# Dummy TensorE products behind the first score products, and another place in the order for the check of two counts

## The chip, the cores and the metric

One core of a Trainium2 chip runs the whole program. The metric is the device time of one execution in microseconds (us): 548.85 us, the median of three runs (548.45 to 549.34).

## The reference

Attention over 2 x 8 heads, 768 tokens, head size 64, with a window: token t sees the first `n_global` (8) tokens and the last `n_local` (96), with a linear bias by distance. Behind it stand two mixture layers on the 1536 x 512 result: `r * (relu(xk W_k)^2 W_v)` with `r = sigmoid(xr W_r)` and `xk`, `xr` mixed from each token and the one before it, then `x + relu(norm(x) W_1) W_2`. All in float32 accuracy; the weights arrive as 64-bit words that the kernel turns into float32 itself.

```python
scores = scale * np.matmul(q, k.transpose(0, 1, 3, 2))
scores = np.where(keep, scores + bias, -1000000000.0)
a = softmax(scores);  x = a @ v
x = r * ((np.maximum(xk @ w_k, 0) ** 2) @ w_v)
return x + np.maximum(norm(x) @ w_ch1, 0) @ w_ch2
```

## The kernel before, in words

The two counts `n_global` and `n_local` are data. The fast path holds for counts up to 8 and 96; `outside_band` (L75 to L88, with `counts`, L64) works out on VectorE (DVE) in small instructions whether they lie outside, and a branch at the very end of the program (L1368 to L1372) reads the flag and would run a general path. `constants` (L249) makes the bias tables from the same counts: a first part for the first block ahead of everything, the rest in four steps (L287 to L298).

The order of the work is not written by hand. Methods of `Fast` hand operations to a planner (`Plan`, L110): each operation has one or more engines with an assumed cost in ns, the cells it reads and writes, the buffers ("rooms") it needs, a due time, and, in `behind`, other operations after which alone it may be placed. `play` (L143) then simulates the engines: again and again it takes, of all operations that could go, the one that can start first, and among those that can start at the same moment the one with the earliest due time (L176). The order that comes out is each engine's instruction queue. On the chip each engine works its queue strictly in that order; `behind` puts no wait of its own into the program, only data and buffers do. So a change of a cost, or one more operation, can change the order of everything planned after it.

The stages, in order of time:

- Attention (to about 133 us). Work goes in half blocks: 128 queries, four heads. `plan_turn` (L431) transposes q and k on TensorE (PE, L446) into PSUM banks 3 and 7; DVE scales q (L453), ScalarE (ACT) copies k (L345). `plan_scores` (L471) makes the scores of a half block with four products (L492) into two of the banks 0 to 2; DVE adds the bias and finds the least value of a row (L503, "least"), ACT takes the exponent (L509). `plan_weighted` (L514) transposes the result (L527), ACT copies it to SBUF (L345), and PE multiplies with v (L542). `plan_out` (L549) scales by the sums: GpSimd (POOL, L566, L570), DVE (L567), PE (L577), ACT (L345), DVE (L583). The scores of half block i are due at 6 + 5 i us of the plan.
- Weight words are converted all along: SP loads (L598), ACT or POOL take the high word (L349, L345), DVE works in L601, L602 and L603, then a high and a low part follow on ACT (L609) and POOL or DVE (L613).
- The first mixture, six groups of 256 tokens: `plan_r` (L728), `plan_k` with the keys products (L764), `plan_v` with the values products (L801 to L803) into banks 4 and 5 (bank 6 in the last group) and DVE L815 that takes them out. `self.mixed` (L937) is the planner's number of the last keys product of the last group.
- The second mixture from about 276 us: `plan_norm` (L834 to L881), `plan_up` (PE L1056, DVE L1064) and `plan_down` (PE L1150 to L1152, DVE L1156 and L1166).

At the start PE has nothing to do until q arrives; `warm_up` (L240) gives it nine products of ones. The check of the counts is the last operation handed to the planner (L942): one DVE operation, cost 3000, no cells, no rooms, nothing in `behind`, and the latest due time of all.

Of the kernel before, what the change touches and what calls it, by code (L numbers as in the profile page):

```python
# [16 lines left out]
P = 128  # L17
B, H, S, D = 2, 8, 768, 64
# [5 lines left out]
NG = NTOK // GT  # L24
# [18 lines left out]
PAIRS = 8  # L43
UP, LEAD = 15.6, 10.0
WARM = 9
SCALE = 0.125
BIG = 2.0**38
SM_EPS = 1e-9
# [3 lines left out]
def slope(h):  # L52
    return 2.0 ** (-8.0 * (h + 1) / H)
# [162 lines left out]
class Fast:  # L216
# [23 lines left out]
    def warm_up(self):  # L240
# [4 lines left out]
        self.nc.vector.memset(y.bitcast(F32), 1.0)  # L245
        for _ in range(WARM):
            self.nc.tensor.matmul(ps, y[:, 0:P], y, start=True, stop=True)
# [52 lines left out]
    def query_scale(self):  # L300
        self.qs = self.t([P, 4, 1], "qs")
        for h in range(H):
            self.nc.gpsimd.memset(self.qs[(h % 2) * D : (h % 2 + 1) * D, h // 2, :], -SCALE / slope(h))

# [166 lines left out]
    def plan_scores(self, i):  # L471


        nc, p = self.nc, self.plan
        n, hf = i // 2, i % 2
        c0, c1 = self.cols(n)
        w = c1 - c0
        banks = [Room(f"b{(2 * i + e) % 3}", 1, lambda e=e: self.bank((2 * i + e) % 3)) for e in range(2)]
        S = lambda k: banks[k % 2].tile[:, 0 : 2 * w].rearrange("p (j w) -> p j w", j=2)[:, k // 2, :]
        due = self.due(i)  # L480
        if hf == 0:
            self.sm[n] = self.room("sm", 3, [P, H])
        sm = self.sm[n]
        tp, mn = self.tp[i], _ = Part([self.TP, self.token(f"tp{i % 3}", 1)], lambda t, _: t[:, i % 3]), self.room("mn", 3, [P, 4])
        sides = [n % 2] if n % NB == 0 else [0, 1, 2]
        o = P + MAXG if n % 2 else 0
        s = hf if n == 0 else 0

        def scores(e):
            for k in range(4):  # L490
                r, c = slice((k % 2) * D, (k % 2 + 1) * D), 2 * hf + k // 2
                nc.tensor.matmul(S(k), self.qT(n)[r, c], self.kT()[r, c, c0:c1], start=True, stop=True)  # L492

        reads = self.sides(n, s, "qT", n % 2)
        for x in sides:
            reads += self.sides(n, s, "kT", x)
        p.op({"PE": 3.4 * w}, scores, reads, [("S", i)], banks + [self.Q, self.K], due, mode="rows")
        for x, k in enumerate((0, 2, 1, 3)):
            h = 4 * hf + k

            def least(e, k=k, h=h):
                bias = self.nb0 if n % NB == 0 else self.nb[:, o : o + WW]
                nc.vector.tensor_tensor_reduce(  # L503
                    tp.tile[:, k, 0:w], S(k), bias, slope(h), 3.0e38, ALU.add, ALU.min, mn.tile[:, k : k + 1]
                )

            def exp(e, k=k, h=h):
                t = tp.tile[:, k, 0:w]
                nc.scalar.activation(t, t, AF.Exp, bias=mn.tile[:, k : k + 1], scale=-1.0, accum_out=sm.tile[:, h : h + 1])  # L509

            p.op({"DVE": 165 + 1.31 * w}, least, [("S", i), ("nb", n % NB > 0)], [("tp", i, k)], [tp, mn, banks[k % 2], self.bias], due + 1 + x)
            p.op({"ACT": 385 + 0.86 * w}, exp, [], [("tp", i, k), ("sm", n, h)], [tp, mn, sm], due + 1.5 + x)

    def plan_weighted(self, i):  # L514

# [367 lines left out]
    def first(self, last):  # L883
        self.plan = p = Plan(CLOCK)
        C = 4 * (2 * P + MAXG)
        self.V, self.sm, self.tp, self.O, self.X, self.k2 = {}, {}, {}, {}, {}, {}
        self.K = self.room("b0h", 1, [P, C + 1024])
        self.Q = self.room("b0l", 1, [P, 4, 512])
        self.U = self.room("u", 1, [P, 2, 512])
        self.VW = self.room("h1", 1, [P, 3, 2, H, D])  # L890
        self.TP = self.room("t0l", 1, [P, 3, 4, GT])
        self.Y = self.room("yy", 1, [P, 2, 2, 512])
        early = self.room("s1", 1, [P, 4, 512, 2], I32)
        bias = self.constants()
        self.bias = Room("ln", 1, lambda: self.nb)
        with self.tc.manual_schedule(engines=ORDERED):
            self.warm_up()
            next(bias)
            self.query_scale()
            self.small_params()  # L900
            rooms = [self.token("rt", 2), self.token("rt", 2), self.token("e", 2)]
            for ns in (350, 500, 800, 900):
                p.op({"DVE": ns}, lambda e: next(bias, None), (), [("nb", True)], rooms, self.due(1))
            for n in range(NBLK):
                self.plan_loads(n)
                self.plan_values(n)
                self.plan_turn(n)
                for i in (2 * n, 2 * n + 1):
                    self.plan_scores(i)
                    self.plan_weighted(i)  # L910
                self.plan_out(n)
            self.plan_weights()
            self.j = 0
            for j, i in enumerate(self.order[0:12]):
                raw = Part([early], lambda t, j=j: t[:, j - 2]) if j in (2, 3) else None
                self.plan_weight(("m1", i), self.src[i], lambda i=i: self.place(i), CONV0 + CONV1 * j, raw=raw)
            for g in range(EG):
                self.plan_r(g, self.due(4 * g + 3) + 45)
            r3 = self.r_op
            self.plan_k(0, K0, K0 - 6)  # L920
            k0 = self.k_op
            for j, i in enumerate(self.order[12:]):
                behind = [r3] if i in (16, 17) else [k0] if i in (14, 15) else []
                self.plan_weight(("m1", i), self.src[i], lambda i=i: self.place(i), CONV2 + CONV3 * j, behind)
            end = self.due(24) + 8
            at = {g: end + 24 * (g - 1) for g in range(NG + 1)}
            self.plan_k(1, at[1], at[1] - 8)
            self.k1 = self.k_op
            self.plan_v(0, at[1] + 12)
            for g in range(1, NG):  # L930
                if g + 1 < NG:
                    self.plan_k(g + 1, at[g + 1], at[g + 1] - 15)
                self.plan_v(g, at[g + 1] + 12 if g + 1 < NG else at[g] + 24)
                if g == 1:
                    self.free = self.x_op
                if g == NG - 2:
                    self.mixed = self.k_op  # L937
                if EG <= g + 1 < NG:
                    self.plan_r(g + 1, at[EG] - 12 + 12 * (g + 1 - EG))
                    self.gone = self.r_op  # L940
            self.plan_second(at[NG])
            p.op({"DVE": 3000}, lambda e: last(), due=at[NG] + 150)  # L942
            self.trace = p.play()

    def plan_second(self, start):
# [451 lines left out]
```

## Time and profile before

| | us |
|---|---|
| median of three runs | 548.85 |
| the profiled execution, as timed | 548.74 |
| its span, first to last instruction | 546.9 |
| PE busy with matmuls | 523.7 |
| DVE busy | 403.0 |
| ACT busy | 288.9 |
| POOL busy | 272.9 |

The span is what the trace covers; the timed execution is 1.84 us longer. Matmuls are pipelined and their ends are modelled, so a busy PE isn't PE at its peak. The page has a row with the clock that TensorE was granted, as a share of 2.4 GHz: it is 1.00 nearly everywhere and 0.50 (1.2 GHz) in one early stretch. On this page the chain that ended last is empty, so what bounds a stage is read from busy times and from what ended an engine's idle time.

### The profile page before, as it was taken

What the parts mean: (1) busy time and instruction counts of PE and PEld (TensorE: products, weight loads), DVE (VectorE), ACT (ScalarE), POOL (GpSimd) and SP (SyncE); (2) the same over time, 40 slices, a digit from 0 to 9 for tenths busy, and PEclk for the clock granted to TensorE, in tenths of its full rate; (3) what the DMA queues carried; (4) which work ended last, traced back from release to release, by engine and by line L of the source; (5) the groups of instructions that cost most, each with busy time, mean ns of one, the idle gap of its engine ahead of it and who ended that gap; (6) DMA issues with size and microseconds to landing.
All of it is one profiled execution on the core that took longest, in us unless ns stands there. A gap on an engine that the chain in (4) does not pass through costs nothing.

```text
span 546.9 us, 8808 instructions
## 1 busy us (share of the span) xinstructions
PE 523.7 (96%) x3177; PEld 454.2 (83%) x3177; DVE 403.0 (74%) x791; ACT 288.9 (53%) x641; POOL 272.9 (50%) x337
## 2 busy tenths in 40 slices
PE   6989999899999999999999999999999999999995
PEld 4667777789899898889789888988889898889983
DVE  6698868995996537459999687786676976679453
ACT  3688988976443225273556364653445544345320
POOL 2277536485754121152256473883855957477200
PEclk9699999999999999999999999999999999999999
DMA  8899875430320000021120204041130312211024
GB/s 159 205 221 167 206 178 146 114 116 5 113 78 0 1 2 0 1 79 43 36 77 1 77 1 132 23 116 39 43 112 1 115 40 81 75 34 44 1 78 159
DMA packets 59568, 42.64 MB, mean 78 GB/s; under 512 B 49148, under 2 KB 49404, under 8 KB 59516
## 3 DMA queue, kind: packets, MB, share of 16 engines
q1 hardware_dynamic: 58796, 41.33, 29.1%
q10 hardware_dynamic: 720, 0.66, 0.4%
q8 instruction: 27, 0.44, 0.3%
q14 instruction: 25, 0.20, 0.1%
HBM read 38.84 MB, written 3.15 MB: 77 GB/s over the span
## 4 chain that ended last, share of the span: by engine, by line


## 5 line engine op out<-in xcount | busy, mean ns | idle before, releaser
L1156 DVE TENSOR_TENSOR xg<-b,xg 128x1024 f32<-128x1024 f32 x44 | 53.7, 1220 | 36.8 <-PE b L1152 36.4
L603 DVE SCALAR_TENSOR_TENSOR cv<-cv,stage 128x512 int32<-128x512 int32 x50 | 44.9, 899 | 12.7 <-ACT cv L345 6.4
L509 ACT ACTIVATE t0l<-t0l,mn 128x232 f32<-128x232 f32 (+1 forms) x96 | 44.4, 467 | 3.5 <-DVE mn L503 3.3
L602 DVE SCALAR_TENSOR_TENSOR stage<-stage 128x512 int32<-128x512 int32 x50 | 43.9, 878 | 0.6
L1075 POOL TENSOR_TENSOR h<-rt,h 128x384 fp32r<-128x384 f32 x28 | 34.0, 1214 | 18.9 <-ACT h L345 18.9
L672 POOL TENSOR_SCALAR rt<-xg,vec 128x256 f32<-128x256 f32 x48 | 31.1, 664 | 20.7 <-DVE yy L779 8.9
L503 DVE CUSTOM_DVE_ANT_0 t0l<-b,ln 128x232 f32<-128x232 f32 (+1 forms) x96 | 31.8, 373 | 9.3 <-PE b L492 9.1
L1075 POOL TENSOR_TENSOR h<-e,h 128x384 fp32r<-128x384 f32 x14 | 15.2, 1089 | 39.1 <-ACT h L345 39.1
L1071 ACT ACTIVATE e<-e 128x384 f32<-128x384 f32 x16 | 8.4, 523 | 49.5 <-DVE e L1064 49.5
L613 POOL TENSOR_TENSOR s<-cv,s 128x384 fp32r<-128x384 f32 (+1 forms) x22 | 25.4, 1156 | 15.4 <-ACT s L609 15.4
L677 DVE SCALAR_TENSOR_TENSOR rt<-xg,vec,rt 128x256 f32<-128x256 f32 x48 | 32.2, 719 | 0.4 <-POOL rt L672 0.3
L764 PE MATMUL b<-b0l,t1l 128*128 128x256 f32 x144 | 32.3, 284 | 0.1
L1071 ACT ACTIVATE rt<-rt 128x384 f32<-128x384 f32 x32 | 16.7, 523 | 27.6 <-DVE rt L1064 27.4
L601 DVE TENSOR_SCALAR stage<-stage 128x512 int32<-128x512 int32 x50 | 30.2, 603 | 1.0 <-DMA stage<-in_moe_w_ch_dram 1.0
L527 PE MATMUL b<-ident,t0l 128*116 128x128 f32 (+1 forms) x176 | 28.3, 284 | 2.5 <-ACT t0l L509 1.7
L542 PE MATMUL b<-yy,h 116*64 116x128 f32 (+1 forms) x352 | 25.4, 286 | 3.1 <-ACT yy L345 3.1
L839 POOL TENSOR_SCALAR st<-st 128x1 f32<-128x1 f32 x12 | 3.7, 308 | 49.2 <-DVE st L836 48.9
L1056 PE MATMUL b<-t0h,s 128*128 128x384 f32 x128 | 27.9, 339 | 0.0
L1056 PE MATMUL b<-t1h,s 128*128 128x384 f32 x128 | 27.8, 338 | 0.0
L492 PE MATMUL b<-b0h,b0l 64*128 64x232 f32 (+1 forms) x192 | 25.8, 389 | 1.6 <-DVE b0l L453 1.0
L542 PEld LDWEIGHTS b<-yy,h 116*64 116x64 f32 (+1 forms) x352 | 19.3, 140 | 9.3 <-ACT yy L345 5.5
L527 PEld LDWEIGHTS b<-ident,t0l 128*116 128x116 f32 (+1 forms) x176 | 19.5, 137 | 8.5 <-issue 3.2
(307 smaller groups left out, 1665.3 us busy)
## 6 DMA issues: line engine op xcount, KB each, us to landing
stage<-in_moe_w_ch_dram SPq DMA_DIRECT2D x32, 512.0 KB
stage<-in_moe_w_k_dram SPq DMA_DIRECT2D x8, 512.0 KB
stage<-in_moe_w_v_dram SPq DMA_DIRECT2D x8, 512.0 KB
h<-in_v_dram SPq DMA_DIRECT2D x10, 192.0 KB
b0l<-in_q_dram SPq DMA_DIRECT2D x7, 256.0 KB
out_dram<-xg SPq DMA_DIRECT2D x3, 512.0 KB
stage<-in_moe_w_r_dram SPq DMA_DIRECT2D x2, 512.0 KB
b0h<-in_q_dram SPq DMA_DIRECT2D x4, 256.0 KB
```

The costliest lines, as they stand in the source:

```text
L503: nc.vector.tensor_tensor_reduce(tp.tile[:, k, 0:w], S(k), bias, slope(h), 3.0e38, ALU.add, ALU.min, mn.tile[:, k : k + 1])
L509: nc.scalar.activation(t, t, AF.Exp, bias=mn.tile[:, k : k + 1], scale=-1.0, accum_out=sm.tile[:, h : h + 1])
L527: nc.tensor.transpose(b.tile[0:w, c, k * P : (k + 1) * P], tp.tile[:, k, c * w : (c + 1) * w], self.ident)
L542: nc.tensor.matmul(o, self.V[n].tile[0:w, c, h, :], y.tile[0:w, c, k * P : (k + 1) * P], start=c == 0, stop=c == m - 1)
L602: p.op({"DVE": 760}, lambda e: nc.vector.scalar_tensor_tensor(low(), high(), -(1 << 31), low(), ALU.bitwise_and, ALU.bitwise_or), [R, (R, ...
L603: p.op({"DVE": 760}, lambda e: nc.vector.scalar_tensor_tensor(y(), y(), 3, low(), ALU.logical_shift_left, ALU.bitwise_or), [(R, 2)], [C], ...
L672: nc.gpsimd.tensor_scalar(y.tile[:, u], z, v, 0.0, ALU.mult, ALU.add)
L677: nc.vector.scalar_tensor_tensor(y.tile[:, u], z, v, y.tile[:, u], ALU.mult, ALU.add)
L764: nc.tensor.matmul(o, l, r, start=s == 0, stop=s == 11)
L1056: nc.tensor.matmul(acc(x), lhs(i, c, n), rhs(r, j, c), start=y == 0, stop=y == 5)
L1075: lambda e: (nc.vector if e == "DVE" else nc.gpsimd).tensor_tensor(o(1), V(y), o(0).bitcast(F32), ALU.subtract),
L1156: p.op({"DVE": 1250}, lambda e, x=x, z=rooms[0]: nc.vector.tensor_tensor(x(), z.tile.rearrange("p a n -> p (a n)"), x(), ALU.add), cells, ...
```

## The change

Two edits. (1) After the score products of half blocks 0, 1, 2 and 3 the planner gets 4, 3, 3 and 2 "fillers": each is two products of the identity with itself into PSUM bank 7, planned at 430 ns, due 2 us after those scores, and placeable once the scores are placed. Nothing reads their result. (2) The check of the counts may be placed only behind the last keys product of the last group.

```diff
+FILL = {0: 4, 1: 3, 2: 3, 3: 2}
...
-        p.op({"PE": 3.4 * w}, scores, reads, [("S", i)], banks + [self.Q, self.K], due, mode="rows")
+        op = p.op({"PE": 3.4 * w}, scores, reads, [("S", i)], banks + [self.Q, self.K], due, mode="rows")
+        for x in range(FILL.get(i, 0)):
+            self.filler(op, due + 2)
...
+    def filler(self, op, due):
+
+
+        b = self.bank_room(7)
+
+        def go(e):
+            for _ in range(2):
+                self.nc.tensor.matmul(b.tile[:, 0:P], self.ident, self.ident, start=True, stop=True)
+
+        self.plan.op({"PE": 430}, go, rooms=[b], due=due, behind=[op])
...
-            p.op({"DVE": 3000}, lambda e: last(), due=at[NG] + 150)
+            p.op({"DVE": 3000}, lambda e: last(), due=at[NG] + 150, behind=[self.mixed])
```

## Rows read from the trace of the kernel before

**Rows 1.** Page, part 1: busy us, share of the span, instructions.

```profile
PE 523.7 (96%) x3177; PEld 454.2 (83%) x3177; DVE 403.0 (74%) x791; ACT 288.9 (53%) x641; POOL 272.9 (50%) x337
```

**Rows 2.** Busy by stretch: length, then each engine; granted clock, DMA share, GB/s.

```profile
5.00:25.00 20.00, 15.46 (x94) 10.69 (x92) 14.58 (x73) 10.36 (x36) 3.40 (x5) 0.74 1.00 205
...
12.20:22.40 10.20, 9.04 (x47) 6.09 (x44) 7.39 (x31) 5.83 (x21) 2.37 (x4) 0.50 0.97 214
25.00:40.00 15.00, 12.30 (x124) 9.23 (x124) 14.52 (x40) 13.25 (x36) 9.27 (x13) 1.00 1.19 223
...
263.00:283.00 20.00, 18.99 (x91) 15.69 (x90) 19.48 (x38) 10.90 (x23) 7.25 (x9) 1.00 0.15 51
283.00:303.00 20.00, 18.95 (x106) 17.18 (x105) 19.84 (x31) 12.02 (x25) 12.93 (x14) 1.00 0.06 18
```

**Rows 3.** Timeline of all engines, 7 to 13 us: start, us, instruction, [idle before].

```profile
7.25 0.41 PE L446 MATMUL b<-ident,u 128*128 128x128 f32 x2 [0.78 <-ACT b0h L345]
...
7.79 0.71 PE L492 MATMUL b<-b0h,b0l 64*128 64x128 f32 x8
7.87 0.16 DVE L67 CAST counts<-words 128x2 f32<-128x2 int32 x1
...
9.61 0.15 DVE L87 CAST flag<-inside 128x1 int32<-128x1 f32 x1
9.68 0.28 DVE L503 CUSTOM_DVE_ANT_0 t0l<-b,ln 128x128 f32<-128x128 f32 x1
...
10.55 0.33 PE L527 MATMUL b<-ident,t0l 128*128 128x128 f32 x1 [1.67 <-ACT t0l L509]
...
10.80 0.71 PE L492 MATMUL b<-b0h,b0l 64*128 64x128 f32 x8
...
11.45 0.66 PE L446 MATMUL b<-ident,b0l 128*128 128x128 f32 x4
...
11.94 0.62 PE L527 MATMUL b<-ident,t0l 128*128 128x128 f32 x3
```

**Rows 4.** PE groups by form, 12.2 to 22.4 us (half clock): busy us, mean ns.

```profile
L492 PE MATMUL b<-b0h,b0l 64*128 64x232 f32 x16 | 3.8, 631 | 0.5 <-ACT b0h L345 0.5
L542 PE MATMUL b<-yy,h 128*64 128x128 f32 x16 | 2.2, 430 | 0.7 <-ACT yy L345 0.7
L527 PE MATMUL b<-ident,t0l 128*128 128x128 f32 x7 | 1.9, 387 | 0.0
```

**Rows 5.** PE groups by form, 22.6 to 60 us (full clock), same columns.

```profile
L527 PE MATMUL b<-ident,t0l 128*116 128x128 f32 x64 | 10.1, 280 | 0.1
L542 PE MATMUL b<-yy,h 116*64 116x128 f32 x112 | 7.7, 279 | 1.7 <-ACT yy L345 1.7
L492 PE MATMUL b<-b0h,b0l 64*128 64x232 f32 x56 | 7.5, 382 | 1.0 <-DVE b0l L453 1.0
```

**Rows 6.** PE timeline, 14 to 24 us, and two idle times of 30 to 40 us.

```profile
16.11 1.92 PE L492 MATMUL b<-b0h,b0l 64*128 64x232 f32 x8 [0.47 <-ACT b0h L345]
...
23.64 0.38 PE L527 MATMUL b<-ident,t0l 128*116 128x128 f32 x2
...
34.10 1.10 PE L542 MATMUL b<-yy,h 116*64 116x128 f32 x16 [1.42 <-ACT yy L345]
...
38.25 1.05 PE L492 MATMUL b<-b0h,b0l 64*128 64x232 f32 x8 [0.96 <-DVE b0l L453]
```

**Rows 7.** Timeline of all engines, 267 to 303 us.

```profile
267.93 0.68 DVE L602 SCALAR_TENSOR_TENSOR stage<-stage 128x512 int32<-128x512 int32 x1
...
272.13 0.67 DVE L815 SCALAR_TENSOR_TENSOR xg<-xg,b 128x512 f32<-128x512 f32 x1
...
272.85 0.50 PE L801 MATMUL b<-s,m 128*128 128x512 f32 x1 [1.01 <-DVE xg L815]
...
276.09 0.94 PE L1056 MATMUL b<-b0h,s 128*128 128x384 f32 x4
...
302.87 0.50 PE L1150 MATMUL b<-b0h,h 128*128 128x512 f32 x1 [1.05 <-DVE xg L1156]
```

## The prediction

> **What bounds the kernel now.** I read the page first: PE is busy 96% of the span and no other engine is over 74% [rows 1], so PE time saved early tends to reach the end, and a PE stall anywhere costs its length. The second view is busy time by stretch [rows 2]. From 5 to 25 us PE is busy 15.46 of 20 and idle 4.54; the granted clock is 0.50 from 12.2 to 22.4 us, so PE there is busy 9.04 us at 1.2 GHz. From 25 to 40 us DVE (14.52 of 15) and ACT (13.25) are the full ones. Much later, 263 to 303 us, DVE is again full (19.48 and 19.84 of 20), while PE has 1.01 and 1.05 us of idle time, both ended by DVE [rows 2, 7]. The third view is the timeline around the two edits. At the start: the first scores start at 7.79 us and run 0.71, to 8.50, but their least (L503) starts only at 9.68, because the check of the counts stands before it on DVE, from 7.87 to 9.76; PE then idles 1.67 us until 10.55 [rows 3]. The clock falls at about 12.2 us; ahead of that PE had this gap and then 1.6 us of transposes and scores.
>
> **The change, part by part.**
>
> *The check leaves the front.* It has no cells, so the planner put it at DVE's first free moment. It takes 9.76 - 7.87 = 1.89 us, less a little for two memsets among it: 1.85. Once it is gone, L503 can start when the scores end: 9.68 - 8.50 = 1.2 us sooner, and with it exponent, first transposes and the second scores (10.80). The other 0.65 us are DVE time that the remaining steps of the bias table can use. No new wait is emitted: `behind` is the planner's alone.
>
> *Half clock.* Same forms at both clocks [rows 4, 5]: L492 16 instructions 3.8 us against 16 x 7.5/56 = 2.14; L542, 16 of them, 2.2 against 16 x 7.7/112 = 1.10; L527, 7 of them, 1.9 against 7 x 10.1/64 = 1.10. Together 7.9 against 4.34, 45% less. On the 9.04 us of the stretch that is 4.1 us of PE time, if the dummies keep the clock at 1.00.
>
> *The dummies.* 12 fillers, 24 products. A float32 product is two instructions here (L492: 4 calls, 8 instructions), so one filler is 4. Nothing in the trace is this product. Bounds: four of L542 at full clock, 4 x 7.7/112 = 0.28 us [rows 5]; four of L446 by themselves with their tail, 0.66 [rows 3]. Nearer rows, start to start: four of L446 take 11.94 - 11.45 = 0.49 and eight of L492 at 128 columns 11.45 - 10.80 = 0.65, or 0.33 for four. I take the middle, 0.41, or 4.9 us for twelve (3.3 to 7.9 with the bounds). At half clock I double it. They wait for no data, but stand in PE's queue: by the planner's rule about two go between the first scores and the first L527, one ahead of the second scores, the others singly among transposes and scores, as each needs bank 7 and a filler's due time is ahead of the next half block's. So a real instruction behind one is late by up to 0.41 us; where PE waits for ACT or DVE anyway, the dummy costs nothing.
>
> *Sum of the front, 5 to 25 us.* PE work: 15.46 - 4.1 + 4.9 = 16.3. Idle: of the 4.54, 0.78 lies ahead of the first scores [rows 3] and stays; the 1.67 shrinks by 1.2 and the dummies fill the rest of it and part of the others; I take 1.5, the 0.78 and as much again for waits that no dummy covers. So 17.8 instead of 20: **2.2 us sooner**. From below: with the dummies at 7.9 and idle 0.78 the work lasts 20.0 and the gain is nothing. From above, by the chain of data: the third scores end at 16.11 + 1.92 = 18.03 [rows 6]; the check takes off 1.2, full clock 0.87 of their own (1.92 against the 1.05 at 38.25) and some 0.5 of the four transposes ahead of them (45% of 1.1), one dummy in the way adds up to 0.41: 15.5 to 15.9, say 15.7, so 2.3 us. The fourth scores give 0.87 again, less what DVE and ACT don't follow: 3.0 at most for the transposes that end at 24.02. DVE allows it: 14.58 - 1.85 = 12.7 us of work in the 17.8. What is late next is ACT's copy of k (the third scores wait 0.47 for it [rows 6]) and, past 25 us, DVE and ACT themselves; both get their inputs earlier, so the gain passes. No DMA is added or moved; the issues on SP's queue that wait for PE or DVE shift with these, and POOL's instructions keep their place.
>
> The Trainium skill (Perfetto Trace Analysis, Identifying the Most-Contended Engine) holds that matmul busy time hides room on TensorE and weight loads show it. PEld is busy only 10.69 of 20 here [rows 2]; by that rule the dummies fit into free room whole, and the front would gain the walk's 3.0 rather than 2.2.
>
> *The check in its new place.* Following the planner's rule through the code's own costs (for order only; no time is taken from them), the first free DVE moment behind the last keys product of the last group is right ahead of the L602 at 267.93 [rows 7]. Behind it queue L602, L603, L774 and the two L815, the last of which (272.13) frees the banks for which PE waits 1.01 us at 272.85 [rows 7]. DVE has next to no idle time until 303, so nothing on DVE hides 1.85 us. Two things on PE can: the planner, seeing banks 4 and 5 late, can put forward up products that were ready (the L1056 at 276.09, four of them 0.94 us [rows 7], and the next group), and after 303 DVE has room, so that weight conversions with later due times can slip there. Bounds 0 and 1.85; I take **0.8 us lost**, somewhat under half for those two covers. If they don't apply, the waits at 272.85 and 302.87 grow to about 2.9 together with what they are now. The flag is read at the very end, 280 us later: no cost.
>
> *Total.* 548.74 for the profiled execution (a span of 546.9 and 1.84 around it, which the change doesn't touch), -2.2 + 0.8 = 547.3; the median shown is 0.11 above that execution, so **547.4 us**. A difference under 0.2% (1.1 us) can't be told from none here.
>
> **The rivals.**
>
> *A. The check's price passes in full.* DVE is full from 263 to 303 and PE's two idle times there end with DVE [rows 2, 7], which speaks for it; that ready up products stand just behind speaks against. Then -2.0 + 1.85: 548.7, no change. Chance 0.22.
>
> *B. The dummies don't stand where the gaps are.* They are only planned; if real work overtakes them in the plan, the clock still falls after the start, and they run later, in time that isn't free. The 1.2 us of the check is gained and mostly paid back at 268: about 548.5. Chance 0.09. Against: their due time is 2 us behind their scores, ahead of all but transposes of the next blocks.
>
> *C. Slower: the clock falls although they are there.* Place: 12 to 22 us on PE. Short gaps remain between groups (ACT's copies, DVE's scaling). For it: the clock fell after groups with one gap of 1.67 us. Against: with gaps of 1.42 and 0.96 us between 30 and 40 us it stayed at 1.00 [rows 2, 6]. Price: four fillers at 0.41 and eight at 0.82, 8.2 us, with nothing saved: 15.46 + 8.2 + 1.5 = 25.2, or 5.2 us later than now, and 0.8 at the check: 554.8. Per us of half clock that remains it is (4.1 + 3.3)/10.2 = 0.7 us, so the forecast's 1.4 is gone once more than 2 us stay at 0.50. Chance 0.08. A rule of the Trainium skill (TensorE: Matmul & The Clock Gate, A second HAM failure mode: psum-queue depth-cycling) would have the clock swing whenever PE stops briefly between groups that cycle through banks, as it does here; the trace bears this out at 12 us and not at 30 to 40.
>
> *D. Another order.* Twelve operations and a moved one change the plan behind them. PE stalls of about 1 us like those at 272.85 and 302.87 [rows 7] can come or go; two more of them where the front gives little make 549.9. Chance 0.08.
>
> **How the numbers follow.** The forecast has 0.53, with its own range 545.6 to 547.7. A and B (0.31) lie within 0.2%; C and D (0.16) are slower. Faster by over 0.2%: 0.53; within: 0.31; slower: 0.16. The range reaches from 545.4 (front 3.0, nothing lost at 268, a stall less) to 549.9 (dummies at 7.9 us, or D); it leaves out C and a little at both ends.
>
> **What would show it.** Right: granted clock 1.00 from 5 to 25 us; the first L503 at about 8.5 us; 48 more PE matmuls, four each in 0.3 to 0.5 us; third scores done near 15.7; transposes that end at 24.02 now near 21 to 22; L67 to L87 past 260 us, followed by a PE wait for L815 no longer than about 2. Wrong: a stretch at 0.50 after 10 us; fillers with waits before them; DVE or ACT that idle for DMA at 13 to 25 us; a gain at 25 us that is gone by 60; or PE waits between 265 and 305 us that grow by the whole 1.85.

## The result, and the profile after

The changed kernel takes 553.85 us (median of 6 runs, 553.07 to 555.99), the kernel before beside it 548.79 (6 runs): a ratio of 1.0103, 95% interval 1.0081 to 1.0125. It is 5.1 us slower, where 1.4 us faster was forecast. The profiled execution took 553.6 us, with a span of 551.8.

The busy times of the page, which answer to [rows 1]:

```profile
PE 528.2 (96%) x3225; PEld 457.1 (83%) x3225; DVE 402.0 (73%) x793; ACT 290.8 (53%) x643; POOL 266.3 (48%) x333
```

PE is busy 4.5 us longer, with 48 instructions more: the dummies, less what the half clock had cost. The span is 4.9 us longer, so PE's idle time has not shrunk, although the gap of 1.67 us at the start is gone. The busy times by stretch, columns as in [rows 2], with one stretch (131 to 185 us) more:

```profile
5.00:25.00 20.00, 19.09 (x159) 15.18 (x158) 15.00 (x65) 12.73 (x43) 4.62 (x7) 1.00 0.95 207
12.20:22.40 10.20, 10.14 (x89) 8.54 (x88) 7.41 (x31) 7.61 (x28) 3.90 (x5) 1.00 0.87 207
25.00:40.00 15.00, 11.62 (x114) 8.81 (x115) 12.02 (x38) 11.13 (x27) 10.63 (x12) 1.00 1.12 227
131.00:185.00 54.00, 52.53 (x340) 46.73 (x339) 42.25 (x60) 24.29 (x43) 28.28 (x34) 1.00 0.15 49
263.00:283.00 20.00, 20.00 (x101) 16.89 (x100) 18.85 (x46) 11.52 (x22) 6.43 (x8) 1.00 0.00 0
283.00:303.00 20.00, 17.12 (x93) 14.62 (x91) 19.21 (x33) 11.75 (x23) 11.09 (x13) 1.00 0.17 54
```

The clock is 1.00 throughout the front, as forecast. PE is almost always busy there (19.09 of 20, 15.46 before), and idles more further on: 3.38 us of the 15 from 25 us on (2.70 before), 1.47 of the 54 from 131 us on, 2.88 of the 20 from 283 us on (1.05 before). The front on the timeline, with the rows that answer to [rows 3] and [rows 6]:

```profile
8.47 0.29 DVE L506 CUSTOM_DVE_ANT_0 t0l<-b,ln 128x128 f32<-128x128 f32 x1
...
8.64 1.38 PE L524 MATMUL b<-ident 128*128 128x128 f32 x8
...
10.72 0.71 PE L493 MATMUL b<-b0h,b0l 64*128 64x128 f32 x8
11.36 0.71 PE L524 MATMUL b<-ident 128*128 128x128 f32 x4
...
15.71 1.05 PE L493 MATMUL b<-b0h,b0l 64*128 64x232 f32 x8
```

Lines have moved down by 1 to 14: L506 was L503, L493 was L492, and L524 is the dummy. The first L506 starts at 8.47 (9.68 before), the third scores end at 16.76 (18.03 before). All dummies in one row of the groups by form (5 to 36 us):

```profile
L524 PE MATMUL b<-ident 128*128 128x128 f32 x48 | 7.9, 288 | 0.2
```

They take 7.9 us of PE, not 4.9: two together take 1.38, one alone 0.61 or 0.71.

To see where time comes and goes I compare the start of the n-th PE instruction (dummies and warm-up left out) with that of the n-th one in the profile of before, and call the difference the lag; a negative one means sooner. Since an order can differ, single values shift by some tenths or more; plateaus count.

| time in before (us) | 24 | 40 | 42 | 131 | 184 to 270 | 278 | 298 | 335 | 449 | end |
|---|---|---|---|---|---|---|---|---|---|---|
| lag of the changed kernel | -1.3 | -2.5 | -0.6 | -1.5 | +1.2 | 0.0 | +3.7 | +1.7 | +4.0 | +4.7 |

So the front gains about what was forecast by 40 us, and three losses follow: at 40 to 42 us, from 131 to 184 us, and from 278 us on. Up to 184 us the orders of the two kernels differ most and the lag swings with them (it is +1.0 at 100 us), so the first two losses are better read from PE's idle times, under run 7. The third, around the check, on the timeline:

```profile
269.03 0.68 DVE L616 SCALAR_TENSOR_TENSOR stage<-stage 128x512 int32<-128x512 int32 x1
269.63 0.15 DVE L68 CAST counts<-words 128x2 f32<-128x2 int32 x1
...
271.36 0.15 DVE L88 CAST flag<-inside 128x1 int32<-128x1 f32 x1
...
274.43 0.68 DVE L829 SCALAR_TENSOR_TENSOR xg<-xg,b 128x512 f32<-128x512 f32 x1
...
286.30 0.63 PE L858 MATMUL b<-ident,ln 128*128 128x128 f32 x4 [1.26 <-DVE ln L862]
...
300.69 0.63 PE L858 MATMUL b<-ident,ln 128*128 128x128 f32 x4 [1.61 <-DVE ln L862]
```

The check stands where the prediction put it, right behind the L602 of before (now L616), and takes 1.80 us (269.63 to 271.43, where the next instruction starts). PE's wait for L815 (now L829), 1.01 us in [rows 7], is gone: PE is busy all the time from 263 to 283 us, as up products were put forward. The wait has moved to the norm: L862 makes what L858 transposes, and PE stands idle 1.26 and 1.61 us for it. Not all of that is DVE's queue. The two L862 themselves take 1.49 and 1.48 us, where L862 takes 0.55 at 275.63; POOL works on L864 beside both, and ahead of the second DVE is idle itself (timeline of the changed kernel):

```profile
275.63 0.55 DVE L862 TENSOR_SCALAR ln<-xg,st 128x512 f32<-128x512 f32 x1
...
284.12 1.75 POOL L864 TENSOR_TENSOR yy<-h,b1h 128x512 fp32r<-128x512 f32 x1 [0.40 <-PE b L817]
284.66 1.49 DVE L862 TENSOR_SCALAR ln<-xg,st 128x512 f32<-128x512 f32 x1
...
299.06 1.48 DVE L862 TENSOR_SCALAR ln<-xg,st 128x512 f32<-128x512 f32 x1 [0.72 <-POOL st L854]
```

### The profile page after: what moved, and what is told of

The parts are those of the page before. It is cut to its first block, busy times and chain, and to the rows that moved or that the text cites. A ratio compares the mean times of both kernels' runs of the same rounds, so it can differ in the third digit from the quotient of the medians.

```text
span 551.8 us, 8908 instructions
## 1 busy us (share of the span) xinstructions
PE 528.2 (96%) x3225; PEld 457.1 (83%) x3225; DVE 402.0 (73%) x793; ACT 290.8 (53%) x643; POOL 266.3 (48%) x333
## 4 chain that ended last, share of the span: by engine, by line
PE 67%; DVE 18%; POOL 5%; issue 4%; ACT 3%; DMA 1%; ACTq 0%; DVEq 0%; POOLq 0%
PE b L1070 12%; PE b L778 11%; PE b L742 6%; PE b L1164 6%; PE b L1166 6%; PE b L1165 6%; PE b L556 3%; PE b L493 3%; PE b L541 3%; DVE xg L1170 3%; DVE stage L616 2%; PE b L817 2%; PE b L816 2%; PE b L815 2%; DVE cv L617 2%
## 5 line engine op out<-in xcount | busy, mean ns | idle before, releaser
L616 DVE SCALAR_TENSOR_TENSOR stage<-stage 128x512 int32<-128x512 int32 x50 | 46.5, 930 | 0.8
L1089 POOL TENSOR_TENSOR h<-rt,h 128x384 fp32r<-128x384 f32 x28 | 31.3, 1116 | 21.9 <-ACT h L346 21.9
L506 DVE CUSTOM_DVE_ANT_0 t0l<-b,ln 128x232 f32<-128x232 f32 (+1 forms) x96 | 32.1, 376 | 11.9 <-PE b L493 11.5
L686 POOL TENSOR_SCALAR rt<-xg,vec 128x256 f32<-128x256 f32 x48 | 28.7, 612 | 23.1 <-DVE yy L793 11.2
L617 DVE SCALAR_TENSOR_TENSOR cv<-cv,stage 128x512 int32<-128x512 int32 x50 | 38.7, 776 | 1.3 <-ACT cv L346 0.3
L615 DVE TENSOR_SCALAR stage<-stage 128x512 int32<-128x512 int32 x50 | 32.3, 647 | 1.5 <-DMA stage<-in_moe_w_ch_dram 1.5
L691 DVE SCALAR_TENSOR_TENSOR rt<-xg,vec,rt 128x256 f32<-128x256 f32 x48 | 30.7, 681 | 2.9 <-POOL rt L686 2.9
L346 ACT ACTIVATE cv<-stage 128x512 f32<-128x512 f32 x38 | 25.1, 664 | 4.6 <-DMA stage<-in_moe_w_ch_dram 2.7
L742 PE MATMUL b<-s,h 128*128 128x512 f32 x96 | 25.9, 405 | 0.9 <-DVE rt L788 0.9
L346 ACT ACTIVATE yy<-b 116x1024 f32<-116x1024 f32 (+1 forms) x24 | 22.8, 948 | 7.1 <-PE b L541 7.0
```

The source lines that it names most:

```text
L346: self.nc.scalar.activation(out, x, AF.Copy, scale=scale)
L616: p.op({"DVE": 760}, lambda e: nc.vector.scalar_tensor_tensor(low(), high(), -(1 << 31), low(), ALU.bitwise_and, ALU.bitwise_or), [R, (R, ...
L617: p.op({"DVE": 760}, lambda e: nc.vector.scalar_tensor_tensor(y(), y(), 3, low(), ALU.logical_shift_left, ALU.bitwise_or), [(R, 2)], [C], ...
L742: nc.tensor.matmul(b.tile, *seq[s], start=s == 0, stop=s == 11)
L1089: lambda e: (nc.vector if e == "DVE" else nc.gpsimd).tensor_tensor(o(1), V(y), o(0).bitcast(F32), ALU.subtract),
```

## The experiments

Beside each group of four runs the kernel before was run again: 549.3, 549.33 and 548.85 us (medians of 31, 30 and 29 runs). Runs of one kernel differ mainly by the mean clock that TensorE was granted, which each run lists, since the stretch at 0.50 comes in some executions and not in others. Of those 90 runs of before, 83 had a clock of 0.980 to 0.989 and 547.97 us or more; five had 0.996 and 546.03 to 546.32. So where terms are added up below, only runs with a clock of 0.996 or more are compared, and their number is given.

Several expectations place the moved check at about 188 or 190 us. In the profiles it starts at 223.45 us (run 4), 218.31 (run 5), 217.60 (run 3), 215.64 (run 7) and 213.49 (run 9).

**1. The check alone.** The dummies are left out; the check stays behind the last keys products.

```diff
-FILL = {0: 4, 1: 3, 2: 3, 3: 2}
+FILL = {}
```

> No fillers; only the check is moved behind the last keys product. Theory O (order: the front gains 2 to 3 us, and a newly planned order gives it back in later stalls): the front gains about 1.2 us, the later order is new again, so anything from -1.5 to +4 us against before, and the lag by stage jumps where no check and no dummy stands. Theory C (the check costs 1.85 us or more in the full DVE stage at 260 to 303 us): a lag of -1 us until 260 us, then +2 or more, end +0.5 to +2. Theory D (the dummies' PE time is the loss): 1 us faster than before, since there are none.

Measured: 551.9 us, ratio 1.0034 (1.0018 to 1.0050). The lag is -2.9 at 24 us, -1.0 at 42 us and -0.2 from 131 to 270 us; then it grows to +2.3 at 298 us and ends at +2.9. The waits that the changed kernel has are here too, on PE's timeline from 262 to 306 us:

```profile
284.92 0.63 PE L858 MATMUL b<-ident,ln 128*128 128x128 f32 x4 [1.27 <-DVE ln L862]
299.32 0.63 PE L858 MATMUL b<-ident,ln 128*128 128x128 f32 x4 [1.62 <-DVE ln L862]
```

The move of the check costs 3.1 us past 270 us, dummies or not: the loss of theory C, half as large again as its 2 us.

**2. The dummies alone.** The check keeps its place at the front.

```diff
-            p.op({"DVE": 3000}, lambda e: last(), due=at[NG] + 150, behind=[self.mixed])
+            p.op({"DVE": 3000}, lambda e: last(), due=at[NG] + 150)
```

> Only the fillers; the check stays at the front. Theory O: the clock stays at 1.00, the front gains 1 to 2 us, later stages lag by a new pattern, end between -2 and +4. Theory C: no loss at 260 to 303 us, end 1 to 2 us faster than before. Theory D: PE has 12 x 0.65 = 7.9 us more and 4.1 less, so a lag of 2 to 4 us at 25 us already that stays to the end.

Measured: 548.54 us, ratio 1.0000 (0.9974 to 1.0026). The lag is -2.3 at 40 us, -1.1 at 42 us and -1.3 to -1.5 from 131 us to the end; the loss between 131 and 184 us isn't there. By itself the dummy edit changes nothing that can be measured: no loss past 260 us, as theory C had it, but no 1 to 2 us of gain either.

**3. Both edits in the old order.** The planner gets the operations of the kernel before. The dummies are issued inside old operations (ten places behind transposes, scores and weighted products of the front), the check inside the second L815 of group 2, at 217.60 us, ahead of an idle time of DVE of 4.48 us that ends at 229.23.

```diff
+                    self.dummies({(0, 0): 1, (0, 3): 2, (1, 3): 1, (2, 0): 1}.get((i, k), 0))
...
+                if g == 2 and tb == 1:
+                    self.last()
...
-            p.op({"DVE": 3000}, lambda e: last(), due=at[NG] + 150)
+            p.op({"DVE": 3000}, lambda e: None, due=at[NG] + 150)
```

> The order of before is held: the twelve dummies are issued inside the operations of the old plan, at about the places they have in the changed kernel, and the check is issued behind the values sums of group 2 (some 188 us), where DVE is idle half the time. Theory O: the front's 2.5 us reach the end, 546 to 547 us, the lag stays near -2.5 at every later stage. Theory C: the same 546 to 547, since the check is out of the full stage. Theory D: slower than before by 2 to 4 us, as the PE time of the dummies is the same.

Measured: 548.34 us, ratio 0.9984 (0.9971 to 0.9996). From 40 us to the end the lag is between +0.2 and +0.5, without a step: all of the changed kernel's later losses are gone. Neither expected time came, the 546 to 547 us or the 2 to 4 us slower: up to 34 us the lag is only -0.6, as the dummies take 8.0 us of PE here. In the profiled execution the clock fell late and took that gain away too. First the idle time ahead of it on PE's timeline, then the clock by stretch:

```profile
33.51 1.09 PE L552 MATMUL b<-yy,h 116*64 116x128 f32 x16 [1.41 <-ACT yy L352]
```

```profile
30.00:34.60 4.60, 3.12 (x41) 2.29 (x37) 4.57 (x16) 4.60 (x16) 2.55 (x4) 1.00 1.10 239
34.60:38.40 3.80, 3.33 (x17) 2.92 (x16) 2.68 (x4) 3.15 (x7) 3.20 (x4) 0.55 1.05 165
```

**4. The check planned behind group 2.** The changed kernel, but the check is behind the DVE step of group 2 (it starts at 223.45 us) instead of the last keys products.

```diff
+                if g == 2:
+                    self.quiet = self.x_op
...
-            p.op({"DVE": 3000}, lambda e: last(), due=at[NG] + 150, behind=[self.mixed])
+            p.op({"DVE": 3000}, lambda e: last(), due=at[NG] + 150, behind=[self.quiet])
```

> The changed kernel, but the check may be placed behind the values sums of group 2 instead of the last keys product; everything planned before about 185 us is the same. Theory C: lag as in the changed kernel until 190 us (+1.2), then no step of 2 us at 280 to 306, end near 550. Theory O: the plan behind 190 us is again another one, so the steps behind move but don't vanish: end 550 to 555. Theory D: as in the changed kernel, 553 to 554.

Measured: 550.65 us, ratio 1.0033 (1.0014 to 1.0052). Up to 171 us the lag is that of the changed kernel within 0.2 us; from 184 us to the end it stays at +0.9 to +1.0, where the changed kernel goes from +1.2 to +4.7. Of PE's idle times from 260 to 305 us one is left on its timeline:

```profile
273.76 0.50 PE L815 MATMUL b<-s,m 128*128 128x512 f32 x1 [0.93 <-DVE xg L829]
```

That is the old wait at 272.85 [rows 7], no longer than before. The place of the check at 268 us costs 3.5 us, as theory C had it.

**5. The reservation without the work.** The planner still places the check at 268 us and keeps 3.0 us of DVE for it, but the instructions are emitted behind the DVE step of group 2 (L829 in the changed kernel, L831 here), at 218.31 us.

```diff
             fn(e)
+            if i == self.at:
+                self.tail()
...
+                if g == 2:
+                    p.at = self.x_op
...
-            p.op({"DVE": 3000}, lambda e: last(), due=at[NG] + 150, behind=[self.mixed])
+            p.tail = last
+            p.op({"DVE": 3000}, lambda e: None, due=at[NG] + 150, behind=[self.mixed])
```

> The changed kernel in its own order, with the 3.0 us that the planner reserves for the check still at 268 us, but the check's 13 instructions emitted behind L829 of group 2, at about 190 us. Theory A (the 1.8 us of VectorE work at 268 us is itself what costs, because VectorE has no free time from 264 to 298 us): the lag against before stays near +1 from 184 us to the end, as with the check planned at 190 us, about 550.6 us. Theory B (the order that the planner makes around its reservation costs, whatever stands there): the lag grows from about +1 at 270 us to +4 to +5 at the end, about 553.5 us. A share of both shows as an end between +2 and +3.5.

Measured: 551.27 us, ratio 1.0039 (1.0026 to 1.0052). The lag is +1.1 up to 270 us and +2.6 at the end, the case of "a share of both". The wait at 286 us is gone, that at 300 us isn't (PE's timeline, 266 to 304 us):

```profile
299.16 0.63 PE L860 MATMUL b<-ident,ln 128*128 128x128 f32 x4 [1.63 <-DVE ln L864]
```

The order made around the reservation costs 1.5 us with no work in it; the other 2.1 us are the work. Where that now stands, PE is busy without a break from 213 to 226 us, and DVE has free time a little later (DVE's timeline):

```profile
218.31 0.16 DVE L68 CAST counts<-words 128x2 f32<-128x2 int32 x1
...
220.05 0.15 DVE L88 CAST flag<-inside 128x1 int32<-128x1 f32 x1
...
229.94 0.89 DVE L866 TENSOR_TENSOR h<-ln,h 128x256 f32<-128x256 f32 x2 [4.47 <-ACT ln L348]
```

**6. The work without the new order.** The kernel before in its own order, the check emitted behind the same L602 (operation 1223 of the plan).

```diff
+            if i == self.at:
+                self.tail()
...
-            p.op({"DVE": 3000}, lambda e: last(), due=at[NG] + 150)
+            p.at = 1223
+            p.tail = last
+            p.op({"DVE": 3000}, lambda e: None, due=at[NG] + 150)
```

> The kernel before, its order kept on every engine and no dummies, with the check's instructions taken from the front and emitted behind the same L602 at 268 us at which they stand in the changed kernel. Theory A (the work itself costs): between 263 and 300 us PE falls back by 3 us or more; with what the front gives (about 1) the end is at +2, 550 to 551.5 us. Theory B (the order costs): it falls back by at most the check's own 1.8 us, and the end is at -1 to +0.8, 547.8 to 549.5 us.

Measured: 550.52 us, ratio 1.0026 (1.0002 to 1.0050). The lag is -1.2 from 24 to 270 us and +0.5 to +0.6 from 278 us to the end: one step of 1.8. In its profiled execution the clock fell for 10.3 us (9.6 to 19.9), about as long as in the kernel before, so -1.2 is what the check's leaving is worth when the clock falls all the same: what the prediction said. The check and the wait behind it on the timeline (L67 to L87 are its first and last instruction, L817 is the L815 of before):

```profile
267.22 0.15 DVE L67 CAST counts<-words 128x2 f32<-128x2 int32 x1
...
268.95 0.15 DVE L87 CAST flag<-inside 128x1 int32<-128x1 f32 x1
...
272.62 0.68 DVE L817 SCALAR_TENSOR_TENSOR xg<-xg,b 128x512 f32<-128x512 f32 x1
...
273.35 0.50 PE L803 MATMUL b<-s,m 128*128 128x512 f32 x1 [2.75 <-DVE xg L817]
```

The check lasts 1.80 us (267.22 to 269.02, the next start), and the wait of 1.01 [rows 7] becomes 2.75. The work passes to PE whole, and nothing later gives it back. By the size of the step both theories' conditions were half met: PE fell back by the check's own 1.8 us and no more, as the second theory has it, and yet that price is real.

**7. Dummies and check behind group 2, in the order of run 2.** The planner reserves the check at the front, as in run 2, so the order is that of run 2; the instructions are emitted behind group 2, at 215.64 us, as in run 5.

```diff
-            p.op({"DVE": 3000}, lambda e: last(), due=at[NG] + 150, behind=[self.mixed])
+            p.tail = last
+            p.op({"DVE": 3000}, lambda e: None, due=at[NG] + 150)
```

> The order of the run with the dummies alone (the planner still reserves the check at the front), the check's instructions emitted behind L829 of group 2, at about 190 us. Theory B (the loss of 2.7 us between 131 and 184 us in the changed kernel is the order that the planner makes when it has both edits): it is gone, the lag stays at -1.3 to -3 from 131 us to the end, 546.3 to 547.5 us and faster than both kernels. Rival (that loss comes from the front's earlier work, which meets the transfers of the weights): it comes back, the end is at 0 to +1, 549 to 550.5 us.

Measured: 547.13 us, ratio 0.9971 (0.9955 to 0.9987); the lag is -1.4 to -1.5 from 131 us to the end. This is run 4 with another order: the same products, and the same check behind the same group, without idle time of PE around it in either. It is 3.5 us faster in the median, 2.7 with the clock kept, and 2.5 us by the lag at the end (-1.4 against +1.0). PE's busy times by stretch, first of run 4 and then of this run, say where:

```profile
25.00:40.00 15.00, 11.76 (x114) 8.95 (x115) 12.21 (x38) 11.24 (x28) 10.64 (x12) 1.00 1.20 229
40.00:60.00 20.00, 19.77 (x164) 15.55 (x163) 17.01 (x52) 17.35 (x49) 16.14 (x22) 1.00 0.93 196
131.00:185.00 54.00, 52.55 (x340) 46.72 (x339) 42.22 (x60) 24.13 (x43) 28.24 (x34) 1.00 0.15 49
```

```profile
25.00:40.00 15.00, 12.69 (x128) 9.72 (x128) 12.71 (x39) 12.04 (x33) 11.58 (x13) 1.00 1.14 228
40.00:60.00 20.00, 19.97 (x162) 15.66 (x162) 17.52 (x56) 17.62 (x50) 14.16 (x20) 1.00 0.94 197
131.00:185.00 54.00, 54.00 (x349) 48.59 (x348) 40.49 (x60) 24.35 (x42) 27.94 (x35) 1.00 0.16 49
```

From 25 to 60 us PE idles 1.1 us more in run 4, and from 131 to 185 us 1.45 us more: together about the 2.5.

**8. One product in a dummy.** As run 7, with the planned 430 ns and so the order kept.

```diff
-            for _ in range(2):
+            for _ in range(1):
                 self.nc.tensor.matmul(b.tile[:, 0:P], self.ident, self.ident, start=True, stop=True)
```

> As the run before it, with one dummy product instead of two at each of the twelve places, the planned 430 ns and so the order kept. If the second product of each pair is what costs (a pair takes 0.61 to 0.71 us in the trace where the prediction had 0.41), a dummy takes 0.25 to 0.35 us and PE runs 3 to 4 us less before 25 us; if that time is on the path, PE's lag at 24 us falls by 1.5 us or more; if the front is set by other engines from 31 us on, the lag at 42 us is the same within 0.3 and the end too. If the dummies carry the clock, a stretch at 0.50 of 3 to 7 us comes back, which is worth 1 to 2 us, about 548.5.

Measured: 545.76 us, ratio 0.9937 (0.9915 to 0.9960), clock 0.996 to 0.999 in all 5 runs. The dummies of run 7 and then those of this run, as one row each of the groups by form:

```profile
L526 PE MATMUL b<-ident 128*128 128x128 f32 x48 | 7.9, 288 | 0.2
```

```profile
L526 PE MATMUL b<-ident 128*128 128x128 f32 x24 | 5.3, 300 | 0.2
```

Twelve products fewer, 2.6 us less of PE (a dummy now takes 0.44 us, more than the 0.25 to 0.35 expected), and the lag falls from -2.3 to -4.5 at 40 us and from -1.5 to -3.9 at 131 to 270 us (it ends at -3.5). The median is 1.4 us lower. So PE's time in the front is on the path, and a dummy there is paid; the single products hold the clock here as the pairs do.

**9. The check moved, no dummies, old order.** The kernel before, with the check emitted as in run 3.

```diff
+                if g == 2 and tb == 1:
+                    self.last()
...
-            p.op({"DVE": 3000}, lambda e: last(), due=at[NG] + 150)
+            p.op({"DVE": 3000}, lambda e: None, due=at[NG] + 150)
```

> The kernel before, its order kept, no dummies, the check's instructions emitted behind L815 of group 2 at about 190 us. Beside the run with the check at 268 us, PE should lie at -1.2 us from 25 us to the end if the 1.85 us of the front lie on the path, with the whole step of +1.8 at 273 us gone: 547.5 us where the clock is as in the kernel before. Rival (the front hides the check): 0 from 42 us on, 548.5 to 549.5 us. Without dummies the front's clock stays open to falls, so a spread of some 545 to 551 us from run to run is expected by both.

Measured: 545.20 us, ratio 0.9955 (0.9926 to 0.9985). The check starts at 213.49 us. The profiled execution has a lag of -3.7 to -3.8 from 24 us to the end, three times what the first theory gave. The ten runs fall into groups by clock: four at 0.996 to 0.998 with 543.8 to 544.0 us, two at 0.995 with 545.1 and 545.3, four at 0.985 or 0.986 with 548.7 to 549.0. So without any dummy the clock is at 0.995 or more in six of ten runs (in 5 of 90 before). But the check's move alone doesn't settle it. In run 6 PE, DVE, ACT and POOL have the same instructions in the same order as here up to 170 us, and only one of its ten runs had 0.995, the other nine 0.977 to 0.989. In the profiled executions of both the clock fell, earlier than in the kernel before and for different lengths (stretches of run 9 first, then of run 6), although PE's idle time ahead of the first transposes of weights (L527) is down from 1.67 us to 0.54 in both:

```profile
9.30:12.70 3.40, 3.31 (x16) 2.46 (x16) 2.43 (x12) 1.65 (x9) 0.63 (x1) 0.50 1.11 224
```

```profile
9.60:19.90 10.30, 9.14 (x46) 6.63 (x48) 6.95 (x30) 4.70 (x19) 1.47 (x3) 0.50 1.11 239
```

On PE's timeline of run 9, 268 to 305 us, the waits are those of [rows 7]:

```profile
269.09 0.50 PE L801 MATMUL b<-s,m 128*128 128x512 f32 x1 [0.94 <-DVE xg L814]
...
299.09 0.50 PE L1156 MATMUL b<-b0h,h 128*128 128x512 f32 x1 [1.02 <-DVE xg L1162]
```

**10. No product at all, order of run 7.** The twelve operations are planned and issue nothing.

```diff
-            for _ in range(2):
-                self.nc.tensor.matmul(b.tile[:, 0:P], self.ident, self.ident, start=True, stop=True)
+            pass
```

> The order of the two runs with dummies and the check at 190 us, no product issued at the twelve places. Theory A (the dummies earn by the clock): a stretch at 0.50 of 3 to 10 us comes back in the first 45 us, and the time is 1 to 4 us above that with one product, 547 to 550 us, with a wider spread. Theory B (the dummies only take PE's time, the kept order and the check's place are what gains): 1.5 to 2.5 us below it, 543.3 to 544.3 us.

Measured: 545.34 us (543.73 to 548.41), ratio 0.9942 (0.9921 to 0.9962). Both theories have a part: the clock is 0.987 to 0.995 in eight of ten runs, and those take 544.5 us and more; the two at 0.997 and 0.998 take 544.61 and 543.73, less than any run with twelve single products.

**11. Single products at every second place** of the order of run 7. The expectation speaks of six; counted by the edit (x is the place behind one half block's scores) they are five.

```diff
-            for _ in range(2):
+            for _ in range(x % 2):
```

> As with one product at each of the twelve places, but only at every second of them, six in all. If six hold the clock as twelve do, PE saves 6 times 0.3, of which about two thirds passed when the pairs were halved (2.4 us of some 3.3): 544.5 us, faster than every kernel so far. If they don't, a stretch at 0.50 shows and the time is 546.5 to 549 us.

Measured: 544.79 us (543.37 to 546.21, 6 runs), ratio 0.9934 (0.9911 to 0.9958): the lowest median, faster than both kernels, though its interval overlaps with those of runs 8, 9 and 10, so which of the four is best stays open. Four of the six runs had a clock of 0.996 or more, two 0.990 and 0.991.

**12. The changed kernel with one product in a dummy**, all else as changed (the diff of run 8).

> The changed kernel, its order and its check at 268 us, one product in each dummy instead of two. If the pair's second product lies on the path there as in the kept order, it ends 2 to 2.6 us earlier than the changed kernel: 551.2 to 551.9 us, still slower than the kernel before. Rival (in the changed kernel's order the front's gain is lost at 40 us to POOL's work, whatever PE did before): the lag at 42 us and the end are as in the changed kernel within 0.5 us, 553.3 to 554.3 us.

Measured: 550.56 us, ratio 1.0040 (1.0020 to 1.0059). The lag is -4.8 at 40 us, -1.2 from 184 to 270 us and +1.4 at the end: at each of them 2.3 to 3.3 us sooner than in the changed kernel, a little more than expected, with the same three losses behind. The rival falls: PE's time in the dummies costs even where POOL's work ends a wait.

## Why the prediction was wrong

The terms, from runs whose clock was 0.996 or more (their number in brackets). Before, as it ran beside the changed kernel, is 548.8; with the clock kept, 546.2 (5). Check out of the front, run 9: 543.9 (4). Dummies in the old order, run 3: 548.2 (6). The new order, check behind group 2, run 4: 549.8 (5). The order around the reservation at 268 us, run 5: 551.3 (10). The check's work there, the changed kernel: 553.4 (4). In steps:

| step | predicted | measured |
|---|---|---|
| clock kept at 1.00 | -4.1 | -2.6 |
| check out of the front | -1.2 | -2.3 |
| dummies, less the idle time that they fill | +4.9, less 1.8 | +4.3 |
| new order from the front to 184 us | 0 | +1.6 |
| check at 268 us: order around it | 0 | +1.5 |
| check at 268 us: its work | +0.8 | +2.1 |
| sum | -1.4 | +4.6 |

The changed kernel's median lies 0.45 us above its runs at 0.996, as two of the six had a clock of 0.991 and 0.992; with it the sum is the 5.1 us measured. The third and fourth step divide in another way if run 7 is put between (547.1 (9): dummies +3.2, order +2.7), because the planner places the dummies better than run 3 does; their sum is +5.9 either way. That a term is the difference of two kernels means that it holds beside the others: with the clock down, the check's leaving is worth less (1.2 us by the lag of run 6; in run 9 548.7 to 549.0 at 0.985 and 0.986, where the kernel before, run beside it, takes 548.8 to 550.1 at 0.985).

*The front was right in its signs, and two of its terms were mis-sized.* The clock (1.00 in the profiled execution), the start of L503 at 8.5 (8.47) and a gain came; the third scores were done at 16.76, not near 15.7. Of the 2.2 us forecast the lag shows 1.3 at 24 us; the 2.5 at 40 us are partly the new order. By the steps above the front's three terms come to -0.6, or to -1.7 with the dummies where the planner puts them. The dummies cost 7.9 us of PE, the upper bound, since each took as long as four L446 alone and not the middle of four rows. The clock's term was too large: two of its three pairs of rows are not of one form (L527 `128*128` against `128*116`, L542 `128*64` against `116*64`). In the changed kernel the very forms of [rows 4] take 2.1 (L492), 1.4 (L527) and 1.3 us (L542) at full clock, 39% less and not 45, and a kept clock gives 2.6 us of time. That the sum of the front is no further off is luck: dearer dummies and a smaller clock term stand against a check that is worth 2.3 us with the clock kept, and not 1.2.

What decides whether the clock falls I had not seen, and it stays open: with the check's move alone it is kept in four of ten runs (run 9) or in none (run 6), with twelve dummies and the check gone from the front in 40 of 53 (the changed kernel, runs 4, 5, 7, 8 and 12). The dummies cost 4.3 us in every execution (3.2 in the planner's order) and save the 4.9 us that a long fall costs in run 9 (548.8 against 543.9) only in those that would have it.

By the rule of the Trainium skill cited in the prediction (Perfetto Trace Analysis, Identifying the Most-Contended Engine), room seen in PEld would have taken the dummies for nothing; PEld is busy 15.18 of 20 with them, and halving them moves the program forward (run 7 to run 8: 2.4 us at 270 us, 2.0 at the end, 1.4 in the median), so the trace does not agree.

*"Both get their inputs earlier, so the gain passes"* is the first step that failed. It passes where the order stays: in runs 3, 6 and 9 the lag is flat from 42 us on, in run 7 from 131 us. In the changed kernel's order it doesn't. The two places, on the timeline of the changed kernel:

```profile
36.94 1.26 POOL L698 TENSOR_TENSOR h<-rt,h 128x512 fp32r<-128x512 f32 x1
...
38.15 1.07 POOL L584 COPY xg<-sm 128x512 f32<-128x512 f32 x1
...
39.28 0.65 PE L591 MATMUL b<-ident,xg 128*128 128x128 f32 x4 [1.40 <-POOL xg L584]
...
138.60 1.51 DVE L691 SCALAR_TENSOR_TENSOR rt<-xg,vec,rt 128x256 f32<-128x256 f32 x1
...
140.04 0.68 DVE L788 SCALAR_TENSOR_TENSOR rt<-b,rt 128x512 f32<-128x512 f32 x1
...
140.77 1.43 PE L742 MATMUL b<-s,h 128*128 128x512 f32 x5 [0.90 <-DVE rt L788]
```

At 39 us PE's queue has the transposes L591 next, which wait for L584 on POOL; in run 7 POOL works in the same sequence (its L584 at 37.97), but PE has another half block's scores ahead of these transposes, and waits only 0.48 us, at 39.75, within these scores. At 140 us PE has the products L742 next, which wait for L788 on DVE, behind two L691 of the other mixture branch, at 137.17 and 138.60; in run 7 this step stands ahead of those two (its L788 at 134.50), and PE has no idle time there. Either is a choice of the plan: the two L691 are as long in run 7 (1.31 and 1.51 us). That the order is the cause is shown (run 4 against run 7), and so is that the time goes at about 40 and at 131 to 185 us, by PE's idle time in the two runs. That it is just these two waits is read from the trace, and no run undid one alone.

*"I take 0.8 us lost" for the check at 268 us* is the second, and so is its upper bound of 1.85. The first cover, up products put forward, came: PE is busy 20.00 of 20 from 263 to 283 us, and the lag even falls to 0.0 at 278. But DVE is busy 19.21 of 20 us up to 303, so what stood behind the check stayed late, and the wait came out at the norm, whose step L862 is also longer there: 1.49 and 1.48 us beside POOL's L864, where the same step (L848) takes 0.93 and 0.75 at 284.87 and 286.18 in the kernel before. How the waits divide between the queue and these longer steps no run shows. The bound left out that the planner reserves 3.0 us and arranges all that follows around them: 1.5 us in run 5. Of these I can point to 0.6: past 305 us PE's waits in run 5 are four of 0.90 to 1.04 us for the step behind the down products (L1156 before), 4.0 with short ones, where the kernel before has five of 0.44 to 0.92, 3.4 in all. The other 0.9 us show as no idle time of PE, and stay open. Run 6 shows what the bound did cover: the work, 1.8 us, entire.

*The rivals.* A, the check's price in full, is what happened and too small by half, since it had the work alone. D, another order, had the mechanism of half of the loss, with a price (two stalls of a us) near the 3.1 measured and too low a chance. "A gain at 25 us that is gone by 60" was on the list of what would show the forecast wrong; the trace shows it later, with a lag of -0.7 at 60 us and +1.2 from 184 us on. B did not come: the dummies stand in the front. C came in part at most: the clock held in four of the six runs, and the two with 0.991 and 0.992 took some 2.5 us longer.

## What to carry to other kernels

A planner that works by simulated times answers every edit with a new order: price an added operation in two parts, its work and the order around its reservation, and tell them apart by emitting the work elsewhere while the plan stays, or by planning it and emitting nothing. Work that no one waits for belongs where its engine has free time soon after (here DVE at 218 us, which then idles 4.47 us ahead of 229.94), not behind the last step of a stage in which its engine is full. And before PE is kept busy with dummies, take away what makes it wait: here that alone (run 9) has a median within 0.6 us of the best versions with dummies (runs 8 and 11), though with a wider spread (543.8 to 549.0, against 545.2 to 545.9 in run 8).

## What the runs showed of the hardware that was not expected

The length of one idle time did not decide whether the clock fell. In run 3 it fell to 0.50 behind 1.41 us of idle time at 33.51 us; in run 9 the same wait was as long, and the clock stayed at 1.00 through the next stretches, as its timeline and its busy times show:

```profile
30.37 1.09 PE L542 MATMUL b<-yy,h 116*64 116x128 f32 x16 [1.41 <-ACT yy L345]
```

```profile
30.00:34.60 4.60, 3.24 (x34) 2.63 (x34) 4.57 (x9) 4.32 (x11) 3.83 (x5) 1.00 1.20 262
34.60:38.40 3.80, 3.80 (x39) 2.86 (x40) 2.39 (x9) 3.29 (x11) 3.80 (x4) 1.00 0.96 150
```

It stayed up with 1.42 us in the kernel before too [rows 6]. And one program meets both in different executions: run 9 took 543.8 us in one run at a clock of 0.996 and 549.0 in another at 0.985, a spread as large as the whole effect of the change. What else decides it no run here shows.

The time of one DVE instruction goes with what POOL does beside it. In the changed kernel the step L691 (128x256, 48 times) takes 0.47 to 0.48 us in the 15 cases in which POOL has no instruction running, and up to 1.53 in the others; L862 takes 0.53 to 0.55 in its seven such cases and 1.49 and 1.48 in the two shown above. A planner with one cost per operation does not see this.

The Trainium skill (TensorE: Matmul & The Clock Gate, A second HAM failure mode: psum-queue depth-cycling) tells of a kernel with bf16 products of 512 columns whose clock swings because PE stops briefly and often between groups that cycle through PSUM banks. The products here are float32. The changed kernel has four stops of 0.72 to 1.40 us between 30 and 65 us at a clock of 1.00, so its trace shows no such swing there; in run 3 the clock did fall behind one.
